# The first contraction block tile by tile, and transposes in PSUM banks of their own

## The chip, the core and the metric

The kernel runs on one core of a Trainium2 chip. The metric is the device time of one execution in microseconds; a kernel's time is the median of its runs. The core's engines run side by side, each with its own queue in program order, and meet at semaphores: TensorE (matmuls and transposes, writing to PSUM), VectorE, ScalarE, GpSimd, and SyncE (SP), which here issues all DMA transfers.

## What is computed

Inputs: x of 2048 rows by 512, and weights, all bf16. Cut to what matters, the reference is:

```python
xn = layernorm(x)
q, k, v = split(xn @ wqkv)                     # 32 heads of 16
# each row attends to 8 rows of its past, 2 apart (0, 2, ... 14 back)
logits = einsum("bhsd,bhswd->bhsw", q, kg) * 16 ** -0.5
s = einsum("bhsw,bhswd->bhsd", softmax(logits), vg) @ wo
h = gelu(xn @ w_gate) * (xn @ w_up)            # 1792 wide
out = x + s * silu(h @ w_down)
```

## The kernel before

The 2048 rows are 16 tiles of 128 rows, and 4 chunks of 4 tiles (`TQ` = 512 columns once transposed). A matmul contracts over 128 partitions, so the 512 features are 4 blocks (`NC` = 4, index `c` or `dk`), and xn is needed transposed: `xnT[j]` holds chunk j as features by rows, 4 blocks by 512 columns.

The order of the work is written out by hand. The program issues each engine's instructions in the order of the Python text, and nothing reorders them; a table of side jobs (`at`, `run`) places work of one stage between the steps of another. For each chunk j the order on TensorE is: 14 pairs of gate and up projections (`glu`), the q, k, v projections of the next chunk (`qkv`), the down projection (`down`), with the attention's sums after its first tile (`sums`: denominators, `av_sums`, then `logits` of the next chunk), and the output projection (`finish`). VectorE multiplies q by k shifted (`qk_products`, tile `pk`), E by v (`av_product`, tile `pv`) and gate by up (`h`, L452). For `av_product` of chunk 0 the v values take a way through DRAM: copied to `vst`, stored to `vT` (L295), and read back as `v_arr` by four transfers (`load_v`, L311), each for 32 of the 128 partitions.

Chunk 0 has a front of its own, which the change touches (L540 to L598):

- Transfers are issued by SP in the order x tiles 0 and 1, three of the four row blocks of wqkv (`load_wqkv`), x tiles 2 and 3, the fourth block, then more of x, and the gate and up weights.
- `first_stats`, `first_moments`, `first_rstd`, `normalize` make xn of a tile on VectorE, with the square root on ScalarE (L191).
- `to_psum` transposes xn's blocks on TensorE (L224) into one PSUM bank (tile `tr`, pool `mm` of four banks), and `from_psum` copies the bank to `xnT`, by ScalarE (L236) for tile 0 and by VectorE for tile 1, in both cases block 0 first and then the other three.
- q, k and v of chunk 0 are made in two halves of 256 columns (`HQ`). The first half (tiles 0 and 1) accumulates in six PSUM banks at once, `pairs`: two banks `v_ps`, and four of the tile `qk_ps`; each bank holds two groups of 128 outputs. These banks are zeroed by matmuls with a zero operand (L545), so that all later products only add. The loop over `dk` (L575 to L584) runs outside: 12 matmuls of 256 columns for each block, with tile 2's transposes behind block 2 and tile 3's within block 3.
- The second half (tiles 2 and 3) follows, one pair of output groups at a time (L594 to L598): `project` runs the four blocks for each of the two groups, and `copy_out` moves the bank to q, k or v.
- `warm_up` issues matmuls whose results are not used.

Of the kernel before, what the change touches and what calls it, by code (L numbers as in the profile page):

```python
# [10 lines left out]
BF16 = mybir.dt.bfloat16  # L11
F32 = mybir.dt.float32

P = 128
# [14 lines left out]
def kernel(  # L29
# [13 lines left out]
    nc = tc.nc  # L43
    B, S, D = A_x.shape
    DF = B_w_gate.shape[1]
    NT, NC, NF, NJ = S // P, D // P, DF // P, S // TQ
# [6 lines left out]
    def pool(name, bufs, **kw):  # L53
        return ctx.enter_context(tc.tile_pool(name=name, bufs=bufs, **kw))
# [19 lines left out]
    mm = pool("mm", 4, space=bass.MemoryType.PSUM)  # L74
# [4 lines left out]
    wqkv_sb = wts.tile([P, NC, 3 * D], BF16, name="wqkv_sb")  # L79
# [7 lines left out]
    def load_x(t, n=1):  # L87
        nc.sync.dma_start(
            out=x_sb[:, t : t + n, :],
            in_=x2d[t * P : (t + n) * P, :].rearrange("(t p) d -> p t d", p=P),  # L90
        )
# [7 lines left out]
    def load_wqkv(k):  # L99
        nc.sync.dma_start(out=wqkv_sb[:, k, :], in_=A_wqkv[k * P : (k + 1) * P, :])  # L100

    for t in (0, 1):
        load_x(t)
    for k in range(NC - 1):
        load_wqkv(k)
    for t in (2, 3):
        load_x(t)
    load_wqkv(NC - 1)
    load_x(TPQ, TPQ)
    for i, (lo, hi) in enumerate(((0, DF // 2), (DF // 2, DF))):  # L110
        load_w(wg_sb, B_w_gate, lo, hi)
# [19 lines left out]
    ident = const.tile([P, P], BF16, name="ident")  # L131
# [38 lines left out]
    xnT = {}  # L170
# [15 lines left out]
    def first_stats(t):  # L186
        nc.vector.bn_stats(out=stats[:, t, :], in_=x_sb[:, t, :])  # L187

    def first_moments(t):
        nc.vector.bn_aggr(out=mv[:, t, :], in_=stats[:, t, :])  # L190
        nc.scalar.activation(  # L191
            out=std[:, t, :], in_=mv[:, t, 1:2], func=AF.Sqrt, bias=epsc[:], scale=1.0
        )

    def first_rstd(t):
        nc.vector.reciprocal(out=rstd[:, t, :], in_=std[:, t, :])
# [9 lines left out]
    xns = {}  # L206

    def normalize(t, cs=range(NC)):
        if 0 in cs:
            xns[t] = xnp.tile([P, D], BF16, name="xn")  # L210
        cols = slice(cs[0] * P, (cs[-1] + 1) * P)
        nc.vector.tensor_scalar(
            out=xns[t][:, cols], in0=x_sb[:, t, cols],
            scalar1=mv[:, t, 0:1], scalar2=rstd[:, t, :],
            op0=ALU.subtract, op1=ALU.mult,
        )

    trs = {}

    def to_psum(t, cs=range(NC)):  # L220
        if 0 in cs:
            trs[t] = mm.tile([P, NC * P], BF16, name="tr", tag="mm")
        for c in cs:
            nc.tensor.transpose(  # L224
                trs[t][:, c * P : (c + 1) * P], xns[t][:, c * P : (c + 1) * P], ident[:]
            )

    def from_psum(t, cs=range(NC), copy=None):
        j, i = divmod(t, TPQ)
        if j not in xnT:  # L230
            xnT[j] = xtp.tile([P, NC, TQ], BF16, name="xnT")
        c = slice(cs[0], cs[-1] + 1)
        dst = xnT[j][:, c, i * P : (i + 1) * P]
        src = trs[t][:].rearrange("p (c n) -> p c n", c=NC)[:, c]
        if copy is None:
            nc.scalar.activation(out=dst, in_=src, func=AF.Copy)  # L236
        else:
            copy(out=dst, in_=src)

    def transpose(t, copy=None):  # L240
        to_psum(t)
        from_psum(t, copy=copy)

    def warm_up(n, cols):

        ps = mm.tile([P, TQ], F32, name="warm_ps", tag="mm")
        for _ in range(n):
            nc.tensor.matmul(
                ps[:, 0:cols], lhsT=nc.const_aps.tensor(1.0, [P, P], BF16),
                rhs=nc.const_aps.tensor(1.0, [P, cols], BF16), start=True, stop=True,  # L250
            )
# [12 lines left out]
    def project(ps, w, lo, j, i0=0, n=TQ):  # L264
        for dk in range(NC):
            nc.tensor.matmul(  # L266
                ps,
                lhsT=w[:, dk, lo : lo + P],
                rhs=xnT[j][:, dk, i0 : i0 + n],
                start=(dk == 0),  # L270
                stop=(dk == NC - 1),
            )
# [3 lines left out]
    def copy_out(j, fo, ps, i0=0, n=TQ, m=1, copy=None):  # L276

        which, c = divmod(fo, NC)
        if which == 0:
            if "q" not in st[j]:  # L280
                st[j]["q"] = qp.tile([P, NC, TQ], BF16, name="q_sb")
            dst = st[j]["q"][:, c : c + m, i0 : i0 + n]
        elif which == 1:
            dst = k_sb[j][:, c : c + m, PAD + i0 : PAD + i0 + n]
        else:
            if c // 2 not in st[j]["vst"]:
                st[j]["vst"][c // 2] = vsp.tile([P, 2, TQ], BF16, name="vst")
            dst = st[j]["vst"][c // 2][:, c % 2 : c % 2 + m, i0 : i0 + n]
        if copy is None:
            nc.scalar.activation(out=dst, in_=ps, func=AF.Copy)  # L290
        else:
            copy(out=dst, in_=ps)
        if which == 2 and (c + m) % 2 == 0 and i0 + n == TQ:
            r, lo = slice((c // 2) * 2 * P, (c // 2 + 1) * 2 * P), PAD + j * TQ
            nc.sync.dma_start(  # L295
                out=vT[r, lo : lo + TQ].rearrange("(c p) n -> p c n", p=P),
                in_=st[j]["vst"][c // 2][:],
            )
# [200 lines left out]
    for i in range(TPQ):  # L499
        at(("down", 0, 1), moments, 2 * TPQ + i)  # L500
        if i < 2:
            at(("glu", 0, i), transpose, TPQ + i)
        at(("down", 0, 2), normalize, 2 * TPQ + i)
        at(("glu", 1, 0) if i else ("down", 0, 3), transpose_by_dma, 2 * TPQ + i)
        at(("glu", 1, 10 + i), moments, 3 * TPQ + i)
        at(("qkv", 2, i), normalize, 3 * TPQ + i)
        at(("glu", 2, 0) if i else ("down", 1, 3), transpose_by_dma, 3 * TPQ + i)
# [31 lines left out]
    HQ = TPQ // 2 * P  # L539
    warm_up(6, TQ // 2)  # L540
    quad = att.tile([P, NC, 2, HQ], F32, name="qk_ps", tag="quad")
    pairs = [(8 + 2 * i, mm.tile([P, 2, HQ], F32, name="v_ps", tag="mm")[:]) for i in range(2)]
    pairs += [(2 * i, quad[:, i]) for i in range(4)]
    for _, ps in pairs:
        nc.tensor.matmul(  # L545
            ps, lhsT=zero[:], rhs=nc.const_aps.tensor(1.0, [P, 2, HQ], BF16),
            start=True, stop=False,
        )
    warm_up(4, P)
    rest = range(1, NC)  # L550
    first_stats(0)
    first_moments(0)
    first_stats(1)
    first_rstd(0)
    first_moments(1)
    normalize(0)
    to_psum(0)
    from_psum(0, [0])
    from_psum(0, rest)
    warm_up(2, P)  # L560
    first_rstd(1)
    normalize(1, [0])
    normalize(1, rest)
    to_psum(1, [0])
    from_psum(1, [0], nc.vector.tensor_copy)
    to_psum(1, rest)
    from_psum(1, rest, nc.vector.tensor_copy)
    for t in (2, 3):
        first_stats(t)
        first_moments(t)  # L570
# [1 line left out]
    for t in (2, 3):  # L572
        first_rstd(t)
        normalize(t)
    for dk in range(NC):  # L575
        for n, (fo, ps) in enumerate(pairs):
            for i in range(2):
                nc.tensor.matmul(  # L578
                    ps[:, i, :],
                    lhsT=wqkv_sb[:, dk, (fo + i) * P : (fo + i + 1) * P],  # L580
                    rhs=xnT[0][:, dk, 0:HQ],
                    start=False,
                    stop=(dk == NC - 1 and i == 1),
                )  # L584
            if (dk, n) in ((2, 5), (3, 2)):
                transpose(dk, copy=nc.vector.tensor_copy)
    for fo, ps in pairs:
        copy_out(0, fo, ps, 0, HQ, 2, nc.vector.tensor_copy if fo >= 8 else None)
    for t in range(TPQ, 2 * TPQ, 2):
# [3 lines left out]
    sum_constants()  # L593
    for n, fo in enumerate((0, 2, 4, 6, 8, 10)):  # L594
        ps = mm.tile([P, 2, HQ], F32, name="qkv_ps", tag="mm")
        for i in range(2):
            project(ps[:, i, :], wqkv_sb, (fo + i) * P, 0, HQ, HQ)
        copy_out(0, fo, ps[:], HQ, HQ, 2)  # L598
    at(("glu", 0, 0), transpose_by_dma, TPQ + 2, (0, 1))
    at(("glu", 0, 0), load_v, 0)  # L600
# [61 lines left out]
```

The softmax here doesn't subtract the row's maximum and nothing guards it: scores larger than these inputs give would overflow.

## Time and profile before

| | us |
|---|---|
| median of 6 runs | 228.74 (228.43 to 228.87) |
| the profiled execution's own time | 228.47 |
| its span, first to last instruction | 226.7 |
| TensorE matmul busy | 221.5 (98%) |
| TensorE weight loads busy | 107.0 (47%) |
| VectorE busy | 152.3 (67%) |
| ScalarE busy | 132.2 (58%) |
| GpSimd busy | 20.1 (9%) |

The profile page cuts the span into 40 slices of 5.67 us; each digit is the busy share of a slice in tenths, for PEclk the granted TensorE clock in tenths of full speed:

```profile
PE   7999999999999999999999999999999999999993
DVE  4689971999995489969812759924934448971434
PEclk9999999999999999999999999999999999999998
DMA  6999399942049911000229931100208940001002
```

In the page PE is TensorE, PEld its weight loads, DVE VectorE, ACT ScalarE, POOL GpSimd, SP the queue that issues transfers. "L224" is line 224 of the kernel before. Matmuls overlap in the pipeline, so one matmul's duration (272 ns at 256 columns) is longer than the spacing from one to the next (109 ns). The DMA row gives the mean busy share of the core's 16 transfer engines: they are saturated for most of the first 23 us, in which the weights and x arrive.

### The profile page before, as it was taken

The page shows a single profiled execution, that of the slowest core. Times are in us where ns is not written, and L with a number is a line of the kernel's source. Part 1 is how long each engine was busy: PE and PEld are TensorE (multiplying, and loading weights), DVE is VectorE, ACT ScalarE, POOL GpSimd, SP SyncE. Part 2 cuts the span into 40 slices and gives each one's busy share as a digit, 9 for nine tenths or more (in the row PEclk, how much of TensorE's full clock was granted, in tenths as well). Part 3 has the DMA queues.
Part 4 walks back from the last instruction along what each step waited for, and adds up shares of the span by engine and source line. Part 5 has one row for each costly group of instructions (what it writes and reads, how often), then busy time and mean ns, then how long its engine had stood idle before and what let it go on. Part 6 is the DMA issues. An engine that isn't in the chain of part 4 may idle for free.

```text
span 226.7 us, 3599 instructions
## 1 busy us (share of the span) xinstructions
PE 221.5 (98%) x1324; PEld 107.0 (47%) x1324; DVE 152.3 (67%) x280; ACT 132.2 (58%) x209; POOL 20.1 (9%) x67
## 2 busy tenths in 40 slices
PE   7999999999999999999999999999999999999993
PEld 3885444444444444444444444444444444444453
DVE  4689971999995489969812759924934448971434
ACT  4478679767631767676751466766763356756210
POOL 1026941000040000320000000000000000000000
PEclk9999999999999999999999999999999999999998
DMA  6999399942049911000229931100208940001002
GB/s 194 386 398 379 71 214 167 320 110 93 7 98 199 194 52 29 19 4 0 93 54 212 180 102 23 26 0 0 91 23 167 200 115 0 0 0 33 0 25 69
DMA packets 30130, 24.64 MB, mean 109 GB/s; under 512 B 10784, under 2 KB 29600, under 8 KB 30112
## 3 DMA queue, kind: packets, MB, share of 16 engines
q1 hardware_dynamic: 30112, 24.41, 44.8%
q8 instruction: 10, 0.16, 0.3%
q14 instruction: 8, 0.07, 0.1%
HBM read 18.74 MB, written 4.34 MB: 102 GB/s over the span
## 4 chain that ended last, share of the span: by engine, by line
PE 96%; DVE 1%; DMA 1%; issue 0%; ACT 0%; DVEq 0%
PE y_ps L460 21%; PE g_ps L266 21%; PE u_ps L266 21%; PE qkv_ps L266 16%; PE s_ps L476 6%; PE L_ps L355 3%; PE o_ps L423 3%; PE qk_ps L578 2%; DMA x_sb<-in_A_x_dram 1%; PE v_ps L578 1%; PE tr L224 1%; DVE stats L187 1%; PE den_ps L375 0%; DVE m L484 0%; DVE mv L190 0%
## 5 line engine op out<-in xcount | busy, mean ns | idle before, releaser
L266 PE MATMUL g_ps<-xnT,wg_sb 128*128 128x512 bf16 x224 | 57.5, 379 | 0.0
L266 PE MATMUL u_ps<-xnT,wu_sb 128*128 128x512 bf16 x224 | 57.5, 379 | 0.0
L460 PE MATMUL y_ps<-wd_sb,h 128*128 128x512 bf16 (+1 forms) x238 | 49.9, 367 | 0.0
L450 ACT ACTIVATE u<-u_ps 128x512 bf16<-128x512 f32 x56 | 33.5, 598 | 16.9 <-PE u_ps L266 16.9
L452 DVE TENSOR_TENSOR h<-ge,u 128x512 bf16<-128x512 bf16 x56 | 23.8, 425 | 29.0 <-ACT u L450 27.3
L448 ACT ACTIVATE ge<-g_ps 128x512 bf16<-128x512 f32 x56 | 33.5, 598 | 16.4 <-PE g_ps L266 16.3
L337 DVE TENSOR_TENSOR pk<-q_sb,k_sb 128x1024 bf16<-128x1024 bf16 (+1 forms) x56 | 38.9, 759 | 4.6 <-ACT k_sb L290 4.6
L409 DVE TENSOR_TENSOR pv<-E,v_arr 128x1024 bf16<-128x1024 bf16 (+1 forms) x48 | 39.7, 862 | 0.0
L266 PE MATMUL qkv_ps<-xnT,wqkv_sb 128*128 128x512 bf16 (+1 forms) x192 | 37.0, 352 | 0.0
L460 PEld LDWEIGHTS <-h 128*128 128x128 bf16 x238 | 23.0, 98 | 25.9 <-issue 1.3
L266 PEld LDWEIGHTS <-wu_sb 128*128 128x128 bf16 x224 | 21.9, 98 | 26.4
L266 PEld LDWEIGHTS <-wg_sb 128*128 128x128 bf16 x224 | 21.7, 98 | 26.3 <-issue 0.8
L468 ACT ACTIVATE sl<-y_ps 128x512 bf16<-128x512 f32 (+1 forms) x17 | 9.7, 572 | 32.6 <-PE y_ps L460 32.6
L266 PEld LDWEIGHTS <-wqkv_sb 128*128 128x128 bf16 x192 | 18.8, 98 | 17.6
L484 DVE TENSOR_TENSOR m<-s_ps,sl 128x512 bf16<-128x512 f32 (+1 forms) x17 | 11.1, 655 | 19.0 <-PE s_ps L476 19.0
L435 DVE TENSOR_TENSOR oT<-o_ps,rb 128x1024 bf16<-128x1024 f32 x8 | 9.4, 1219 | 11.8 <-DMA rb<-rs_d 6.3
L476 PE MATMUL s_ps<-wo_sb,oT 128*128 128x512 bf16 (+1 forms) x68 | 14.8, 366 | 0.0
L204 POOL TENSOR_TENSOR rstd<-rstd,mhalf 128x1 f32<-128x1 f32 x12 | 8.1, 671 | 71.2 <-DVE rstd L201 71.2
L290 ACT ACTIVATE vst<-qkv_ps 128x512 bf16<-128x512 f32 x14 | 8.4, 597 | 3.7 <-PE qkv_ps L266 3.7
L290 ACT ACTIVATE k_sb<-qkv_ps 128x512 bf16<-128x512 f32 x14 | 8.4, 601 | 3.2 <-PE qkv_ps L266 3.2
L290 ACT ACTIVATE q_sb<-qkv_ps 128x512 bf16<-128x512 f32 x14 | 8.3, 603 | 3.0 <-PE qkv_ps L266 3.0
L476 PEld LDWEIGHTS <-oT 128*128 128x128 bf16 x68 | 6.6, 98 | 7.2
(58 smaller groups left out, 126.4 us busy)
## 6 DMA issues: line engine op xcount, KB each, us to landing
v_arr<-vT SPq DMA_DIRECT2D x16, 520.0 KB, 8.6
vT<-vst SPq DMA_DIRECT2D x8, 256.0 KB, 2.5
out_dram<-o_t SPq DMA_DIRECT2D x15, 128.0 KB, 2.5
wg_sb<-in_B_w_gate_dram SPq DMA_DIRECT2D x2, 896.0 KB, 9.9
wu_sb<-in_B_w_up_dram SPq DMA_DIRECT2D x2, 896.0 KB, 10.8
wd_sb<-in_B_w_down_dram SPq DMA_DIRECT2D x1, 1792.0 KB, 10.7
wqkv_sb<-in_A_wqkv_dram SPq DMA_DIRECT2D x4, 384.0 KB, 4.7
x_sb<-in_A_x_dram SPq DMA_DIRECT2D x3, 512.0 KB, 9.8
```

The costliest lines, as they stand in the source:

```text
L266: nc.tensor.matmul(ps, lhsT=w[:, dk, lo : lo + P], rhs=xnT[j][:, dk, i0 : i0 + n], start=(dk == 0), stop=(dk == NC - 1),)
L290: nc.scalar.activation(out=dst, in_=ps, func=AF.Copy)
L337: nc.vector.tensor_tensor(out=st[j]["pk"][w][:, c0 : c0 + n, :], in0=st[j]["q"][:, c0 : c0 + n, :], in1=k_sb[j][:, c0 : c0 + n, off : off ...
L409: nc.vector.tensor_tensor(out=pv[:, d : d + n, :], in0=st[j]["E"][:, wh, :].unsqueeze(1).to_broadcast([P, n, TQ]), in1=st[j]["va"][:, 4 * ...
L435: nc.vector.tensor_tensor(out=oT[:, g : g + 2, :], in0=st[j]["o"][:, g : g + 2, :], in1=st[j]["rb"][:].unsqueeze(1).to_broadcast([P, 2, TQ ...
L448: nc.scalar.activation(out=ge[:], in_=g_ps[:], func=AF.Gelu_apprx_tanh)
L450: nc.scalar.activation(out=u[:], in_=u_ps[:], func=AF.Copy)
L452: nc.vector.tensor_tensor(out=h[:], in0=ge[:], in1=u[:], op=ALU.mult)
L460: nc.tensor.matmul(y[:], lhsT=st[j][fc][:, tt * P : (tt + 1) * P], rhs=wd_sb[:, fc, cols], start=(fc == 0), stop=(fc == NF - 1),)
L468: nc.scalar.activation(out=sl[:], in_=y[:], func=AF.Silu)
L476: nc.tensor.matmul(s[:], lhsT=st[j]["oT"][:, g, tt * P : (tt + 1) * P], rhs=wo_sb[:, g, cols], start=(g == 0), stop=(g == NC - 1),)
L484: nc.vector.tensor_tensor(out=m[:], in0=s[:], in1=sl[:], op=ALU.mult)
```

## The change

The products of block 0 are made for tile 0 alone and then for tile 1 alone, 128 columns each, in place of 256 columns at once. They are put between the transposes of tile 1. To that end tile 0's normalization is split like tile 1's was, and block 0's transposes of both tiles go into one PSUM bank (`tra`), those of the other three blocks into another (`trb`). Two unused matmuls go. The transposes of tiles 2 and 3 move to later places in block 3. The first pair of output groups of the second half is made tile by tile too. The load loop is written out with the same transfers in the same order.

```diff
-    for t in (0, 1):
-        load_x(t)
-    for k in range(NC - 1):
-        load_wqkv(k)
-    for t in (2, 3):
-        load_x(t)
-    load_wqkv(NC - 1)
+    load_x(0)
+    load_x(1)
+    load_wqkv(0)
+    load_wqkv(1)
+    load_wqkv(2)
+    load_x(2)
+    load_x(3)
+    load_wqkv(3)
...
-    def to_psum(t, cs=range(NC)):
-        if 0 in cs:
-            trs[t] = mm.tile([P, NC * P], BF16, name="tr", tag="mm")
-        for c in cs:
+    def to_psum(t, cs, tr):
+        for n, c in enumerate(cs):
             nc.tensor.transpose(
-                trs[t][:, c * P : (c + 1) * P], xns[t][:, c * P : (c + 1) * P], ident[:]
+                tr[:, n * P : (n + 1) * P], xns[t][:, c * P : (c + 1) * P], ident[:]
             )
...
+    def block(dk, ns, i0=0, n=HQ):
+        for b in ns:
+            fo, ps = pairs[b]
+            for i in range(2):
+                nc.tensor.matmul(
+                    ps[:, i, i0 : i0 + n],
+                    lhsT=wqkv_sb[:, dk, (fo + i) * P : (fo + i + 1) * P],
+                    rhs=xnT[0][:, dk, i0 : i0 + n],
+                    start=False,
+                    stop=(dk == NC - 1 and i == 1),
+                )
+
+    one, rest = [0], range(1, NC)
+    tra = mm.tile([P, 2, P], BF16, name="tra", tag="mm")
+    trb = mm.tile([P, 2, (NC - 1) * P], BF16, name="trb", tag="mm")
     first_stats(0)
     first_moments(0)
     first_stats(1)
     first_rstd(0)
     first_moments(1)
-    normalize(0)
-    to_psum(0)
-    from_psum(0, [0])
-    from_psum(0, rest)
-    warm_up(2, P)
+    normalize(0, one)
+    to_psum(0, one, tra[:, 0])
+    from_psum(0, one, tra[:, 0])
+    normalize(0, rest)
+    to_psum(0, rest, trb[:, 0])
+    from_psum(0, rest, trb[:, 0])
     first_rstd(1)
-    normalize(1, [0])
+    normalize(1, one)
     normalize(1, rest)
-    to_psum(1, [0])
-    from_psum(1, [0], nc.vector.tensor_copy)
-    to_psum(1, rest)
-    from_psum(1, rest, nc.vector.tensor_copy)
+    block(0, range(2), 0, P)
+    to_psum(1, one, tra[:, 1])
+    from_psum(1, one, tra[:, 1], nc.vector.tensor_copy)
+    block(0, range(2, 6), 0, P)
+    to_psum(1, rest, trb[:, 1])
+    from_psum(1, rest, trb[:, 1], nc.vector.tensor_copy)
+    block(0, range(6), P, P)
...
-    for dk in range(NC):
-        for n, (fo, ps) in enumerate(pairs):
-            for i in range(2):
-                nc.tensor.matmul(
-                    ps[:, i, :],
-                    lhsT=wqkv_sb[:, dk, (fo + i) * P : (fo + i + 1) * P],
-                    rhs=xnT[0][:, dk, 0:HQ],
-                    start=False,
-                    stop=(dk == NC - 1 and i == 1),
-                )
-            if (dk, n) in ((2, 5), (3, 2)):
-                transpose(dk, copy=nc.vector.tensor_copy)
+    block(1, range(6))
+    block(2, range(6))
+    block(3, range(3))
+    transpose(2, nc.vector.tensor_copy)
+    block(3, range(3, 5))
+    transpose(3, nc.vector.tensor_copy)
+    block(3, range(5, 6))
...
     for n, fo in enumerate((0, 2, 4, 6, 8, 10)):
         ps = mm.tile([P, 2, HQ], F32, name="qkv_ps", tag="mm")
-        for i in range(2):
-            project(ps[:, i, :], wqkv_sb, (fo + i) * P, 0, HQ, HQ)
+
+        w = HQ if n else P
+        for i0 in range(0, HQ, w):
+            for i in range(2):
+                project(ps[:, i, i0 : i0 + w], wqkv_sb, (fo + i) * P, 0, HQ + i0, w)
         copy_out(0, fo, ps[:], HQ, HQ, 2)
```

## The prediction

> **What bounds the kernel.** I read the chain of waits first, by line and in order of time, then the timeline of the first 13 us for each engine, then TensorE's later waits. TensorE carries the end:
>
> ```profile
> PE 96%; DVE 1%; DMA 1%; issue 0%; ACT 0%; DVEq 0%
> ```
>
> It can therefore be shortened only before TensorE's stream starts, or where the stream pauses. The chain in order of time shows the start of the stream (start us, us, what):
>
> ```profile
> 5.25 0.33 DVE xn L212
> 5.57 0.04 issue
> 5.62 0.24 PE tr L224
> 5.86 0.02 issue
> 5.89 0.24 DVE xnT L238
> 6.12 0.04 issue
> 6.17 0.33 PE tr L224 x3
> ...
> 59.34 1.77 PE L_ps L355 x32
> ...
> 113.24 1.73 PE L_ps L355 x32
> ```
>
> Up to 6.17 TensorE serves as one link in tile 1's chain: normalize, transpose, copy, transpose. The first product starts at 6.33 in the timeline, behind all transposes of tiles 0 and 1. From there every step of the chain is TensorE's. So the change is worth what its stream of first products gains on the present one, less what a later stage takes back. For the latter, note that the logits of chunk 1 (L_ps at 59.34) take 1.77 us and those of chunk 2, the same 32 instructions, 1.73.
>
> **The front, step by step.** Durations are those of the early timeline and of the groups by shape.
>
> Tile 0. Its normalization starts at 4.60 as now. In place of one 128x512 operation (382 ns) comes a 128x128 one, then 128x384. Tile 1 has both shapes: 314 and 374 ns, the second starting 0.23 after the first. The first ends at 4.92. TensorE starts 0.05 after its data (4.98 to 5.04 now) and a transpose takes 0.23: 4.97 to 5.20. Now ScalarE's copy waits for all four:
>
> ```profile
> 5.04 0.40 PE L224 MATMUL tr<-ident,xn 128*128 128x128 bf16 x4 [0.53 <-DVE xn L212]
> ...
> 5.48 0.66 ACT L236 ACTIVATE xnT<-tr 128x128 bf16<-128x128 bf16 x2 [0.46 <-PE tr L224]
> ```
>
> (start us, us, engine, line, operation, out<-in, shape, count, idle time before; 5.04 + 0.40 = 5.44, copy at 5.48.) With block 0 in its own bank it waits for one: 5.24, 278 ns, 5.52. The first product follows at **5.57**, for 6.33 now. Its weights landed at 1.71 + 3.3 = 5.0.
>
> From there TensorE runs 4 products, 1 transpose, 8 products, 3 transposes, 12 products before block 1: 28 instructions of 128 columns. Their spacing is the price that decides. In the fence above four transposes, each with a weight load of its own, take 0.40 with a single one at 0.23: (0.40 - 0.23)/3 = 0.056. So 28 x 0.0555 = 1.55, and block 1 starts at 7.13. Now it starts at 7.64 (6.33 + 12 x 0.109). **Gain 0.51.**
>
> Waits inside, each against its slot: rstd of tile 1 is pushed by the extra VectorE operation from 5.05 to about 5.13, so xn block 0 of tile 1 ends at 5.64 and the rest at 5.93. TensorE comes to that transpose at 5.80 (cover 0.1; without it 0.08 is lost). Its copy ends at 6.29, wanted at 6.46. ScalarE's second copy ends at about 6.11, wanted at 6.30 by tile 1's other transposes. Their copy ends at 6.63 + 0.04 + 0.36 = 7.03, wanted at 7.13: the tightest, 0.05 after the signal. Weights of blocks 1, 2, 3 land at 6.6, 7.6, 9.2, wanted at 7.13, 8.44, 9.74. The stall at 6.17, 0.32 behind VectorE's copy of the shared bank, and the wait for four transposes both go; what is late next is TensorE itself. The two removed warm-ups (0.11) lie in an idle stretch, and the pause before the transposes shrinks. The load loop written out issues the same eight transfers.
>
> Tiles 2 and 3. Their normalization ends at 10.15 and 10.67 as now (the x tiles land at 7.9 and 8.3). TensorE gets to tile 2 at 7.13 + 30 x 0.109 = 10.39 and to tile 3 at 10.39 + 0.22 + 0.44 = 11.05, so the later places cover the earlier stream. Then 2 products end at 11.49. The first group pair starts with tile 2, whose copy ends at 10.82 + 0.42 = 11.24. Tile 3's copy ends at 11.47 + 0.42 = 11.89, its part starts at 11.94. As one 256-column pair it would wait until 11.94 to start at all, 0.45 lost; that is what the split is worth. It has 16 instructions of 128 columns for 8 of 256: 0.89 for 0.87. The next pair starts at 12.40 where now it is 12.91: **0.51 stays**. ScalarE's copies shift along. VectorE's next stretch moves only 0.09, as its casts follow tile 3's copy, but at 25.5 it waits for ScalarE's u (0.23 idle), and the last pk before the first L_ps ends at 32.27 with TensorE there at 33.36: covered.
>
> **Where part of it stops.** The transfers do not move. The last quarter of v_arr is issued at 28.09 and:
>
> ```profile
> DMA to landing us min/median/max: 12.0/12.0/12.0
> ```
>
> It lands at 40.1, and the first pv starts at 40.27:
>
> ```profile
> 39.93 0.43 DVE L452 TENSOR_TENSOR h<-ge,u 128x512 bf16<-128x512 bf16 x1 [0.55 <-ACT u L450]
> 40.27 1.22 DVE L409 TENSOR_TENSOR pv<-E,v_arr 128x2048 bf16<-128x2048 bf16 x1
> 41.41 0.42 DVE L452 TENSOR_TENSOR h<-ge,u 128x512 bf16<-128x512 bf16 x1
> 41.74 1.22 DVE L409 TENSOR_TENSOR pv<-E,v_arr 128x2048 bf16<-128x2048 bf16 x1
> 43.01 0.43 DVE L452 TENSOR_TENSOR h<-ge,u 128x512 bf16<-128x512 bf16 x1
> 43.35 1.22 DVE L409 TENSOR_TENSOR pv<-E,v_arr 128x2048 bf16<-128x2048 bf16 x1
> 44.73 0.43 DVE L452 TENSOR_TENSOR h<-ge,u 128x512 bf16<-128x512 bf16 x1 [0.17 <-ACT u L450]
> 45.08 5.76 DVE L409 TENSOR_TENSOR pv<-E,v_arr 128x2048 bf16<-128x2048 bf16 x5
> 50.75 9.71 DVE L337 TENSOR_TENSOR pk<-q_sb,k_sb 128x1024 bf16<-128x1024 bf16 x16
> ```
>
> With h half a us earlier, pv still has to wait for 40.1. From 40.27 VectorE can go at its own pace: pv to h 1.14, h to pv 0.33. That gives h at 41.41, 42.88, 44.35 and the run of five pv at 44.69 for 45.08. The pk behind it have no gap, so the last ends at 60.07 for 60.46 (50.75 + 9.71): **0.39 earlier, no more**. The 28th of the 32 L_ps instructions needs it, and TensorE waits there by 0.04 already (1.77 against 1.73). So TensorE cannot leave that stage more than 0.39 earlier, and everything behind follows it. The transfer's own range: the two vT rows that v_arr waits for are issued at 17.2 and 18.1, would be issued 0.5 earlier, and take 7.1 and 7.9 us to land, where chunk 1's take 2.8 and 4.0. They queue behind the input loads; if so, nothing moves. At the other end they move by the full 0.5, for which speaks that the transfers' share between 23 and 26 us is only 0.26. I take 0, as the queueing is the larger part. SP gets no other order.
>
> **Rule against row.** The Trainium skill, "TensorE: Matmul & The Clock Gate", section on the back-to-back issue gap, says that in streams of weight load and matmul pairs 128 columns cost about 81 ns each, not 56. The change makes 12 pairs of 256 columns into 24 of 128 and 8 into 16, so it adds the overhead of 20 instructions and must not pay more than half a 256-column slot each. By the row the 40 short ones cost 40 x 0.0555 = 2.22, by the rule 3.24. The rule takes the 0.51 away and adds another 0.5. The row has loads at the same spacing through six instructions (transposes and warm-ups, 5.05 to 5.33), so a load hides behind a 128-column matmul. I take the row. The load's own 98 ns is the far end.
>
> **Sum.** Profiled execution: 228.47, span 226.7 (1.77 around it). Span 226.31, time 228.08. Against the median, 228.74 - 0.39 = **228.35**.
>
> **Rivals.**
> - *All comes through*: v_arr lands earlier with its vT rows, or in most executions. Then 0.51 + the 0.04 of the present wait: 228.20. For it: half-idle transfers before 26. Against: the saturated queue up to 23.
> - *Little comes through*: v_arr lands 0.3 to 0.4 later than in this one profile. Then pv binds before and after alike: 228.6 to 228.74. For it: the six runs spread 0.44. Against: nothing in the change adds transfers. The same time results if the products start late because a copy is waited for as a whole (first product at 6.16, block 1 at 7.7).
> - *Slower*: short pairs bound by weight loads. At 81 ns 40 x 0.0255 = +1.02, less 0.51, less the 0.04 wait that then vanishes: 229.2. At 98 ns +1.70: 229.9. It decides from 0.0555 + 0.55/40 = 69 ns per pair. Against it stands the row above; for it that no run of more than six such loads is in the trace.
>
> **Chances.** A difference of 0.2% is 0.46 us, about what can be told from no change. Main case 0.42 (0.25 to 0.5 gained, 228.25 to 228.5; about a third of it beyond 0.46), all comes through 0.32, little 0.11, slower 0.15. Faster 0.15 + 0.29 = 0.44, same 0.42, slower 0.14. Range 228.0 to 229.0: it takes in the first three and leaves out most of the slower one.
>
> **What would show it.** First v_ps product near 5.57 and block 1 near 7.13; 128-column products spaced 55 to 57 ns; the second pair of the second half near 12.40; pv not before 40.2 with idle VectorE ahead of it; L_ps of chunk 1 at 1.85 to 1.9 us. Wrong if the short products are spaced over 69 ns, if v_arr moves with TensorE, or if a wait appears between 7 and 12 us.

## The result and the profile after

| kernel | runs | median us | lowest to highest | ratio to the kernel before, 95% interval |
|---|---|---|---|---|
| before | 40 | 228.76 | 228.35 to 229.39 | 1 |
| after | 20 | 228.13 | 227.79 to 228.61 | 0.9976 [0.9970, 0.9982] |

By the ratio, the changed kernel is 0.55 us faster (0.41 to 0.69); the medians lie 0.63 apart. The forecast was 228.35, a gain of 0.39. This lies just below the interval; the rival "all comes through" (0.51 to 0.55) lies in it.

The profiled execution of the changed kernel took 228.35 with a span of 226.6, only 0.12 less than the profiled execution of before (228.47, 226.7). So this pair of profiles shows a fifth of what the medians show, and the first question was where the rest is. The chain of waits, by engine:

```profile
PE 98%; DVE 0%; issue 0%; DVEq 0%
```

It was 96% with 1% each for VectorE and DMA: nearly the whole chain is TensorE's own work. In order of time (start us, us, what), read from the profiled execution of after:

```profile
4.84 0.43 PE warm_ps L245 x4
5.26 0.11 PE tra L221
5.37 0.43 PE trb L221 x3
5.80 0.32 PE v_ps L551 x4
6.12 0.06 PE tra L221
6.17 0.45 PE qk_ps L551 x8
6.62 0.17 PE trb L221 x3
...
10.52 0.22 PE qk_ps L551 x2
10.74 0.02 issue
10.76 0.40 PE tr L221 x4
...
59.21 1.77 PE L_ps L352 x32
```

Three readings. First, normalization and copies no longer appear between the first transposes and the products: the stall ahead of tile 1's transposes is gone. Second, the four warm-ups take 0.43 and the three transposes behind them 0.43, where three later ones take 0.17. TensorE ran at half its rate until shortly before the first product. The two timelines show it too, first before, then after (start us, us, engine, line, operation, out<-in, shapes, count):

```profile
2.92 1.36 PE L545 MATMUL qk_ps<-const-bfloat16-1.0,zero 128*128 128x512 bf16 x4
4.12 0.40 PE L248 MATMUL warm_ps<-const-bfloat16-1.0 128*128 128x128 bf16 x4
```

```profile
2.92 1.91 PE L542 MATMUL qk_ps<-const-bfloat16-1.0,zero 128*128 128x512 bf16 x4
4.63 0.63 PE L245 MATMUL warm_ps<-const-bfloat16-1.0 128*128 128x128 bf16 x4
```

The same four zeroing matmuls, which the change leaves alone, take 1.36 in one execution and 1.91 in the other, so the difference is one between executions. Third, tile 2's transposes start at 10.76, 0.18 after TensorE is free (an "issue" of 0.02 stands in the chain; the timeline shows the gap): tile 2 of x landed at 8.48 in this execution and at 7.92 in the one of before. Both chances fell on the changed kernel. A second profiled execution of each kernel, the two on one chip, makes another pair (the clock's rise is read from the trace's record of the granted clock):

| times in us | before | before, second | after | after, second |
|---|---|---|---|---|
| TensorE's clock rises to full | 3.6 | 5.2 | 5.7 | 4.2 |
| x tile 2 landed | 7.92 | 8.27 | 8.48 | 8.35 |
| first product | 6.33 | 6.37 | 5.74 | 5.54 |
| block 1 starts | 7.64 | 7.68 | 7.31 | 7.12 |
| second pair of second half starts | 12.91 | 13.21 | 12.78 | 12.64 |
| v_arr landed | 40.13 | 40.26 | 39.19 | 39.89 |
| first pv starts | 40.27 | 40.57 | 40.14 | 40.02 |
| L_ps of chunk 1 starts | 59.34 | 59.64 | 59.21 | 59.07 |
| span | 226.74 | 227.06 | 226.62 | 226.49 |

Read down the second and fourth columns: 0.57 is gained by the second pair, 0.57 is still there at L_ps, and 0.57 in the span. In the first and third columns it is 0.13, 0.13 and 0.12. Nothing that is gained or lost in the front is given back later, in either pair. Neither pair is quite even: in the second one chance favours the changed kernel, as the clock rises earlier in it and tile 2's transposes wait for their rows for 0.15, for 0.25 in before.

TensorE's timeline of the second execution of after, for the steps that were predicted:

```profile
5.54 0.40 PE L551 MATMUL v_ps<-xnT,wqkv_sb 128*128 128x128 bf16 x4
...
7.12 0.60 PE L551 MATMUL v_ps<-xnT,wqkv_sb 128*128 128x256 bf16 x4
...
10.63 0.40 PE L221 MATMUL tr<-ident,xn 128*128 128x128 bf16 x4
...
11.30 0.39 PE L221 MATMUL tr<-ident,xn 128*128 128x128 bf16 x4
...
11.74 1.50 PE L263 MATMUL qkv_ps<-xnT,wqkv_sb 128*128 128x128 bf16 x20
```

From the first product to block 1 it is 1.58 for 28 instructions of 128 columns: 56 ns each. In the first pair of the second half, 16 short instructions from 11.74 to 12.64 give 56 again.

And VectorE's timeline of the same execution, where the prediction saw the gain capped:

```profile
39.66 0.43 DVE L449 TENSOR_TENSOR h<-ge,u 128x512 bf16<-128x512 bf16 x1 [0.56 <-ACT u L447]
40.02 1.23 DVE L406 TENSOR_TENSOR pv<-E,v_arr 128x2048 bf16<-128x2048 bf16 x1
...
44.47 0.42 DVE L449 TENSOR_TENSOR h<-ge,u 128x512 bf16<-128x512 bf16 x1 [0.17 <-ACT u L447]
44.81 5.76 DVE L406 TENSOR_TENSOR pv<-E,v_arr 128x2048 bf16<-128x2048 bf16 x5
```

The first pv starts 0.36 after h starts. In before it is 0.34, so a wait for v_arr can be 0.02 at most. The brackets name ScalarE's u as what VectorE waited for, still as in before. The cap did not bind.

### The profile page after: what moved, and what is told of

Same layout as the page of the kernel before. It is cut to its first block, busy times and chain, and to the rows that moved or that the text cites. A ratio compares the mean times of both kernels' runs of the same rounds, so it can differ in the third digit from the quotient of the medians.

```text
span 226.6 us, 3637 instructions
## 1 busy us (share of the span) xinstructions
PE 222.3 (98%) x1342; PEld 107.6 (47%) x1342; DVE 152.3 (67%) x281; ACT 132.3 (58%) x209; POOL 21.4 (9%) x67
## 4 chain that ended last, share of the span: by engine, by line
PE 98%; DVE 0%; issue 0%; DVEq 0%
PE y_ps L457 21%; PE g_ps L263 21%; PE u_ps L263 21%; PE qkv_ps L263 16%; PE s_ps L473 6%; PE L_ps L352 3%; PE o_ps L420 3%; PE qk_ps L551 2%; PE warm_ps L245 1%; PE v_ps L551 1%; PE qk_ps L542 1%; PE tr L221 0%; PE den_ps L372 0%; PE v_ps L542 0%; PE trb L221 0%; DVE m L481 0%
## 5 line engine op out<-in xcount | busy, mean ns | idle before, releaser
L263 PE MATMUL qkv_ps<-xnT,wqkv_sb 128*128 128x512 bf16 (+2 forms) x200 | 37.0, 345 | 0.0
```

The costliest lines, as they stand in the source:

```text
L263: nc.tensor.matmul(ps, lhsT=w[:, dk, lo : lo + P], rhs=xnT[j][:, dk, i0 : i0 + n], start=(dk == 0), stop=(dk == NC - 1),)
```

## The experiments

Two theories were held against each other. By the **stream** theory, the gain is the front's (a product stream that starts earlier and stays dense), and it reaches the end. By the **landing** theory, the landing of v_arr cuts it off near 0.39; the expectations call this the cap theory. Four kernels, u1 to u4, undo one part of the change each, the v and c kernels move the landing, and i1 tries to go further. Each ratio is to runs of before taken beside the kernel: their median was 228.73 for a0 and u1 to u3, 228.79 for u4, v1, v2 and i1, and 228.55 for c0, c1, a1 and b1. No kernel puts back the two removed matmuls by themselves.

**The changed kernel again, beside its parts (a0).** No edit.

> The changed kernel once more, as it is, for a second profile of it. Stream theory (the start of TensorE's stream sets the end and nothing later takes any back): 0.50 to 0.55 us under the kernel before. Cap theory (v_arr's landing near 40 us holds pv, and the L_ps of chunk 1 gives back what is over 0.39): 0.35 to 0.40 under it, L_ps of chunk 1 at 1.85 us or more. Clock theory (in the first profile of the changed kernel the TensorE clock rose at 5.7 us where in that of before it rose at 3.6, which is chance of the execution): with a rise before 4.5 us the first product lies near 5.57 and block 1 near 7.13; with a late rise near 5.75 and 7.3.

Measured: 228.22 (11 runs), ratio 0.9981 [0.9972, 0.9989], a gain of 0.43 (0.25 to 0.64). Its first product came at 5.73 and its second half started at 11.82, with the clock's rise at 6.1. The two measurements of the changed kernel overlap; 0.39 is in this interval and 0.51 too. The medians of one kernel alone do not tell the two theories apart.

**Block 0 whole (u1).** The banks, the split of tile 0 and the split pair stay; the products of block 0 wait for both tiles.

```diff
-    block(0, range(2), 0, P)
     to_psum(1, one, tra[:, 1])
...
-    block(0, range(2, 6), 0, P)
     to_psum(1, rest, trb[:, 1])
...
-    block(0, range(6), P, P)
+    block(0, range(6))
```

> Block 0 again in products of 256 columns behind all transposes of tile 1; banks, split normalization, later transposes and the pair by tiles stay. Stream theory: tile 1's three transposes share a bank with tile 0's and wait for ScalarE's second copy (6.11), so block 0 starts at 6.3 and block 1 at 7.6 as before: no gain, 0.5 us slower than the changed kernel, ratio to before 1.000. If instead the banks and the later transposes bring the gain by themselves, it stays 0.4 to 0.5 under the kernel before.

Measured: 228.54, ratio 0.9994 [0.9986, 1.0002], not told apart from before: 0.14 of the gain is left, 0.32 at most. TensorE's timeline:

```profile
5.59 0.22 PE L221 MATMUL tra<-ident,xn 128*128 128x128 bf16 x1
6.13 0.33 PE L221 MATMUL trb<-ident,xn 128*128 128x128 bf16 x3 [0.32 <-ACT xnT L232]
6.30 0.60 PE L551 MATMUL v_ps<-xnT,wqkv_sb 128*128 128x256 bf16 x4
...
7.61 0.60 PE L551 MATMUL v_ps<-xnT,wqkv_sb 128*128 128x256 bf16 x4
```

The first product is back at 6.30 and block 1 at 7.61, beside 6.33 and 7.64 in before. The 0.32 of idle time is there again under another name: in before VectorE's copy of tile 1's block 0 held the shared bank, here it is ScalarE's copy of tile 0's other blocks, which uses the same bank trb. In the changed kernel the products of the first tile lie in this gap. So in this profile the new banks bring the products no earlier unless the first tile's products stand between the transposes.

**Banks by tile (u4).** Everything of the change stays but the layout: one bank for each tile in place of one for block 0 and one for the rest.

```diff
-    tra = mm.tile([P, 2, P], BF16, name="tra", tag="mm")
-    trb = mm.tile([P, 2, (NC - 1) * P], BF16, name="trb", tag="mm")
+    tr0 = mm.tile([P, NC * P], BF16, name="tr0", tag="mm")
+    tr1 = mm.tile([P, NC * P], BF16, name="tr1", tag="mm")
...
-    to_psum(0, one, tra[:, 0])
+    to_psum(0, one, tr0[:, 0:P])
...
-    to_psum(0, rest, trb[:, 0])
+    to_psum(0, rest, tr0[:, P:])
```

> The transposes of each tile again in a bank of the tile's own (four blocks in one bank) in place of block 0 and the others apart; the order of all instructions stays as in the changed kernel. Stream theory: tile 0's other transposes wait for ScalarE's copy of block 0 (5.57), tile 1's others for VectorE's (6.55), so block 1 starts near 7.4 in place of 7.13: half of the gain stays, 0.25 under the kernel before. If the banks don't matter: 0.5 to 0.55 under it.

Measured over 21 runs: 228.40, ratio 0.9989 [0.9982, 0.9995], a gain of 0.25 (0.11 to 0.41): about half of the whole change. TensorE's timeline shows the place:

```profile
5.73 0.38 PE L221 MATMUL tr<-ident,xn 128*128 128x128 bf16 x3 [0.37 <-ACT xnT L232]
5.95 0.39 PE L551 MATMUL v_ps<-xnT,wqkv_sb 128*128 128x128 bf16 x4
```

The three other transposes of tile 0 wait 0.37 for ScalarE's copy of block 0 from the same bank, and the first product starts at 5.95 behind them, beside 5.54 to 5.74 in the changed kernel. The split and the banks are two halves of one thing. In every kernel here a tile of transposes fills a bank of its own, so no run tells whether it is the bank or the tile that is waited for.

**The first pair whole (u2).**

```diff
-        w = HQ if n else P
+        w = HQ
```

> The first pair of output groups of the second half again with 256 columns; all else of the change stays. Stream theory: the pair waits for tile 3's copy at 11.94 in place of 11.49; TensorE idles 0.45 us there, the kernel stays 0.05 to 0.1 under the one before. Cap theory: the loss against the changed kernel is only 0.3, as that one has 0.39 at most to lose. If tile 3's copy is not late, no loss.

Measured: 228.48, ratio 0.9996 [0.9988, 1.0004], a gain of 0.09 left, 0.27 at most. TensorE's timeline:

```profile
11.75 0.38 PE L551 MATMUL qk_ps<-xnT,wqkv_sb 128*128 128x256 bf16 x2
12.43 1.80 PE L263 MATMUL qkv_ps<-xnT,wqkv_sb 128*128 128x256 bf16 x15 [0.30 <-DVE xnT L234]
```

Two products from 11.75 at 0.109 end at 11.97, and the pair starts at 12.43, behind VectorE's copy of tile 3: 0.46 lost, where the prediction had 0.45. With a later place for the transposes and no split, most of the front's gain is lost at the seam, where the second half begins.

**Transposes at their old places (u3).** Tile 2 goes back ahead of block 3, tile 3 to behind three pairs of it.

```diff
-    block(3, range(3))
     transpose(2, nc.vector.tensor_copy)
-    block(3, range(3, 5))
+    block(3, range(3))
     transpose(3, nc.vector.tensor_copy)
-    block(3, range(5, 6))
+    block(3, range(3, 6))
```

> Tile 2's transposes again behind block 2 and tile 3's behind the third pair of block 3; all else of the change stays. Stream theory: TensorE reaches tile 2's transposes at 9.74, its normalized rows are there at 10.20 (x lands at 7.9, later in the first profile of the changed kernel, 8.5), so it idles 0.45 to 0.9 us: 0 to 0.1 under the kernel before, or above it by up to 0.3 where x lands late. If x of tile 2 is early enough in most executions, no loss.

Measured: 228.64, ratio 0.9998 [0.9989, 1.0006].

```profile
10.20 0.40 PE L221 MATMUL tr<-ident,xn 128*128 128x128 bf16 x4
...
11.96 1.28 PE L263 MATMUL qkv_ps<-xnT,wqkv_sb 128*128 128x128 bf16 x18
```

In this execution x came early enough that TensorE waited only 0.09 for tile 2, and the second half started at 11.96 with the clock's rise at 6.2, within 0.14 of the changed kernel's 11.82 at 6.1. The profile thus shows less of a loss than the runs do, by whose ratio most of the gain is lost (0.05 left, 0.25 at most). In the executions with later x, this order waits longer: before has the same places, and its second execution waited 0.25 there. That this makes up the whole difference is argued from the landings, not measured.

**The landing taken away (v1 on before, v2 on after).** Chunk 0's v is read from x, an input, in place of the stored vT, so that its transfers wait for no store. Chunk 0's attention output is then not the reference's.

```diff
-                    tensor=vT.tensor,
+                    tensor=vT.tensor if j else A_x.tensor,
...
-                    ap=[[SV * DH, H], [SV, DH], [1, VW]],
+                    ap=[[(SV if j else S - PAD) * DH, H], [SV if j else S - PAD, DH], [1, VW]],
```

> The kernel before, with chunk 0's v_arr read from the input x in place of the stored v (same rows and bytes; so chunk 0's attention output is not the reference's). It does not wait for the stored v and lands some 3 us sooner, near 37. Both theories: the kernel before waits for v_arr only in executions where it lands after 40.2; if that is rare, ratio 1.000; if it is frequent, up to 0.1 us faster.

> The changed kernel with the same: chunk 0's v_arr read from x (chunk 0's attention output is not the reference's), landing near 37. Cap theory: the cap goes, 0.1 to 0.15 us faster than the changed kernel, 0.55 and more under the kernel before. Stream theory (v_arr is in time in most executions): same as the changed kernel within 0.05.

Measured: v1 228.68, ratio 0.9996 [0.9988, 1.0004]; v2 228.06 (6 runs), ratio 0.9971 [0.9959, 0.9982]. v_arr landed at 38.05 and 37.66, some two us sooner than in before, where three were expected. In before that is worth nothing that can be measured. In the changed kernel it is worth 0.0005 of the ratio against the first measurement and 0.001 against the second (0.1 to 0.2 us), inside the intervals. So if the landing takes a part of the gain at all, it is a small one.

v2's profile is also the cleanest front of all: clock's rise at 4.3, x tile 2 at 7.96, first product 5.41, tile 2's transposes at 10.25 without a wait, second pair at 12.26, span 226.10. Against before's second pair at 12.91 that is 0.65, and the spans differ by 0.64. (0.13 of it is tile 0 of x, which landed at 2.83 and not at 2.96.)

**The landing delayed (c0 on before, c1 on after).** SP's queue is reordered so that v_arr of chunk 0 is issued behind more of the transposing transfers.

```diff
-    at(("glu", 0, 0), transpose_by_dma, TPQ + 2, (0, 1))
+    at(("glu", 0, 0), transpose_by_dma, TPQ + 2)
+    at(("glu", 0, 0), transpose_by_dma, TPQ + 3, (0, 1))
     at(("glu", 0, 0), load_v, 0)
-    at(("glu", 0, 0), transpose_by_dma, TPQ + 2, (2, 3))
-    at(("glu", 0, 0), transpose_by_dma, TPQ + 3)
+    at(("glu", 0, 0), transpose_by_dma, TPQ + 3, (2, 3))
```

> The kernel before, with four of the six DMA transposes of tiles 6 and 7 ahead of chunk 0's v_arr transfers in place of behind them, so that v_arr is issued some 2 us later. Cap theory (pv waits for v_arr, and from there VectorE's chain to the L_ps of chunk 1 holds TensorE): with the last quarter landing at A, the first pv is at A + 0.14, the run of five pv 4.4 later, and TensorE waits before or in L_ps of chunk 1 for what this exceeds 45.1; for a landing at 41.5 some 0.9 us slower than the kernel before. If TensorE does not depend on it: ratio 1.000.

> The changed kernel with the same move. Cap theory: both are bound by v_arr, whose landing does not follow TensorE, so the gain is gone: the same time as the kernel before with this move, within 0.15 us. If TensorE does not depend on v_arr's landing, or the landing follows TensorE's earlier start: 0.5 us under that one, as without the move.

Measured: c0 230.67 (6 runs, 229.73 to 231.84), ratio 1.0096 [1.0069, 1.0123]; c1 229.88 (5 runs, 229.60 to 230.13), ratio 1.0057 [1.0044, 1.0070]. VectorE's timeline of c0, then of c1:

```profile
41.95 1.23 DVE L409 TENSOR_TENSOR pv<-E,v_arr 128x2048 bf16<-128x2048 bf16 x1 [1.65 <-DMA v_arr<-vT]
...
46.37 5.75 DVE L409 TENSOR_TENSOR pv<-E,v_arr 128x2048 bf16<-128x2048 bf16 x5
```

```profile
42.08 1.22 DVE L406 TENSOR_TENSOR pv<-E,v_arr 128x2048 bf16<-128x2048 bf16 x1 [1.81 <-DMA v_arr<-vT]
...
46.50 5.76 DVE L406 TENSOR_TENSOR pv<-E,v_arr 128x2048 bf16<-128x2048 bf16 x5
```

Now the bracket ahead of pv names the transfer. In both kernels pv starts 0.12 after the landing (41.83, 41.96), the run of five pv follows 4.42 later as predicted, and TensorE waits in L_ps: from den_ps to the next y_ps it takes 5.07 and 5.24, where every other profile has 3.73. TensorE's timeline of c0 shows the waits:

```profile
59.11 1.87 PE L355 MATMUL L_ps<-pk,dsum 128*32 128x512 bf16 x26
61.20 0.38 PE L355 MATMUL L_ps<-pk,dsum 128*32 128x512 bf16 x1 [0.23 <-DVE pk L337]
61.81 0.59 PE L355 MATMUL L_ps<-pk,dsum 128*32 128x512 bf16 x5 [0.23 <-DVE pk L337]
```

The chain of c0's page:

```profile
PE 80%; DVE 10%; DMA 6%; SPq 2%; issue 1%; ACT 0%; DVEq 0%; ACTq 0%
```

VectorE and the DMA have come into it. Span minus landing is 186.2 in both, so in this pair of executions the front's gain is gone and the landing alone sets the end. So the cap is real as a mechanism. The medians do not show the two kernels equal within 0.15, as they should be under a binding landing: 0.79 lies between them, with few runs and intervals that just touch. The traced execution of c0 (229.73) is the fastest of its six, and the median is 2.1 above that of before where 0.9 was expected of a landing at 41.5. Only one execution of each has a trace, so whether the landings differ by as much in the others stays open.

**x sooner (i1).** An attempt to go further: tiles 2 and 3 of x are loaded ahead of the third block of wqkv, so that tile 2's transposes need not wait.

```diff
     load_wqkv(1)
-    load_wqkv(2)
     load_x(2)
     load_x(3)
+    load_wqkv(2)
     load_wqkv(3)
```

> The changed kernel with x tiles 2 and 3 loaded ahead of wqkv's third block. They land some 1.0 us sooner, the third block 0.7 later (7.8 to 8.3, wanted at 8.4). If TensorE waits for tile 2's rows in many executions (0.18 idle at 10.76 in the first profile of the changed kernel), 0.1 to 0.2 us faster than the changed kernel and 0.6 to 0.75 under the one before; if that was chance, the same as the changed kernel; if the third block is late, slower by up to 0.3.

Measured: 228.58 (13 runs, 228.0 to 231.65, the slowest not in the ratio), ratio 0.9996 [0.9984, 1.0007]: 0.09 of the gain is left, 0.37 at most. Tile 2's transposes did not wait (11.10, straight behind the products). But the execution profiled has the latest clock rise of all, 6.8, and the first product itself waited for its weights, as the weight loads (LDWEIGHTS) show:

```profile
5.79 0.35 PEld L551 LDWEIGHTS <-wqkv_sb 128*128 128x128 bf16 x4 [0.27 <-DMA wqkv_sb<-in_A_wqkv_dram]
```

The first block of wqkv landed at 5.75, although it is issued ahead of what was moved. The third landed at 8.74; here block 2 starts at 9.13, but in an execution like the second one of after it would be wanted near 8.4 and TensorE would wait some 0.3. Whether that is what the runs show, or the late first block is, stays open.

**Both kernels profiled again (b1, a1).** No edit; their numbers are in the table above.

> The kernel before as it is, for a second profile of it. Clock theory (the moment at which the TensorE clock rises is chance of the execution): with a rise after 5 us, its first product lies near 6.6 and its span near 227.0, where the first profile, with a rise at 3.6, has 6.33 and 226.7. If the rise is a property of the kernel, it is at 3.6 again.

> The changed kernel as it is, for a third profile. With a rise of the clock before 4.5 us: first product 5.4 to 5.6, block 1 near 7.0 to 7.1, span near 226.1. With a late one: 5.75, 7.3 to 7.5, 226.5. v_arr's last quarter: near 39.2 again if its landing follows the stores of v, 39.1 to 40.1 if it is chance.

Measured: 228.79 and 228.19, one execution each, 0.60 apart; spans 227.06 and 226.49. The fronts are 0.57 apart, and so are the ends. Single executions scatter: 11 runs of before beside these two have a median of 228.55. Two expectations missed. In b1 the clock rose at 5.2 and the first product came at 6.37, not near 6.6; its span of 227.06 comes from the wait of 0.25 for tile 2. In a1 the span is 226.49, not 226.1, in part as TensorE waited 0.07 for block 3's weights (landed at 9.76) and 0.15 for tile 2. With v_arr at 39.89 in a1, pv started 0.13 after it, where c0 and c1, which do wait, have 0.12: here the landing only just did not bind.

## Why the prediction was right, and where it was not

- **The start.** First product predicted at 5.57; 5.54 with an early clock rise, 5.73 and 5.74 with late ones. Right for executions whose clock rises early; the prediction took the clock of one execution as given.
- **The spacing.** Predicted 55 to 57 ns; 56 in 28 and in 16 instructions in a row. The row of four transposes held for long runs, and the rival "slower", which decides from 69, falls. By the rule of 81 (the Trainium skill, "TensorE: Matmul & The Clock Gate", back-to-back issue gap) block 1 would have started, as an estimate, at 5.54 + 28 x 0.081 = 7.81; it started at 7.12.
- **Tiles 2 and 3.** Transposes predicted at 10.39 and 11.05 with no wait; measured 10.63 and 11.30 in a1, with a wait of 0.07 for block 3's weights (they landed at 9.76, not at 9.2) and one of 0.15 for tile 2; the first profile has 0.18 for tile 2. "A wait between 7 and 12 us" was named as a sign against the forecast. It came, because tile 2 of x landed at 8.35 and 8.48 and not at 7.92. It takes little of the gain, as before waits too when x is late (0.25 in its second execution). In v2, where x landed at 7.96, there is no wait.
- **The seam** between the halves. The split of the first pair was put at 0.45; undoing it (u2) left 0.46 idle. Second pair predicted at 12.40; measured 12.64 and 12.78, and 12.26 in v2. Against before the difference is 0.13 and 0.57 in the two pairs. The most alike executions are v2 and the first of before: 0.65, and 0.52 without the 0.13 of tile 0's earlier landing, where 0.51 was forecast.
- **The cap: the mis-sized term.** The sum took 0.39 of the 0.51, since v_arr lands at 40.13, and "I take 0" for what its landing moves. The mechanism is right: c0 and c1 show pv tied to the landing, 4.42 to the run of five, and TensorE waiting in L_ps. The size was taken from one landing in one execution. In three executions of the changed kernel v_arr landed at 39.14 to 39.89. With the latest of these the cap lies at 0.39 + (40.13 - 39.89) = 0.63, above what the front brings. The first pv came at 40.02 to 40.14 and L_ps of chunk 1 took 1.77, where "not before 40.2" and 1.85 to 1.9 were named as signs. The traces show the way: v_arr's first transfer is issued 0.06 to 0.07 after the last vT row has landed, at 25.02 to 25.55 in the three and at 25.70 and 25.98 in before. That row is issued a little earlier in the changed kernel (17.83 to 17.97, for 18.10 and 18.40), but its time to land differs between executions of one kernel by as much (7.05 to 7.72, and 7.30 and 7.88). How much of the earlier landing is the change's and how much chance stays open.
- **A small one.** The rival "all comes through" added 0.04 for a wait that TensorE has in L_ps now. In v2 v_arr landed at 37.66 and L_ps of chunk 1 still took 1.78: that 0.04 is not a wait for v_arr.

So the direction, the spacing and the front's sum were right, and the case that came is the rival in which all comes through. It was luck that the clock and the landings of x, which the sum took from one execution, mattered little to the difference of the medians: each moves a single execution by some 0.2 to 0.3. The range of 228.0 to 229.0 takes in no change at all too, so that 228.13 lies in it says little; the traces carry the argument.

## What to carry to other kernels

Where one engine's stream sets the end, a stream that starts half a us earlier is worth half a us only if each later seam is moved with it: undoing any one of three edits lost most of the gain. Before a transfer's landing is used as a cap, look at a second execution: it moved here by more than the margin that decided. The same goes for a comparison of profiles, where one pair showed 0.12 and another 0.57 of a change that the ratio puts at 0.55.

## What the runs showed of the hardware

**TensorE's clock rises at a time of its own.** In fourteen profiles of this program and its variants the rise lay between 3.6 and 6.8 us after the start, although TensorE's work begins at 0.83 or 0.84 in all of them and is the same in its first 12 matmuls, the last of which starts at 3.9 to 4.2. Until it, 128-column matmuls are 107 ns apart, and 56 after it. The record of the clock starts at the rise, so the clock row of the page shows a 9 from its first slice on, and the slow start is seen only in the early timeline. In the kernel before, a rise at 5.7 (v1) goes with a first product at 6.62 and a span of 227.04, one at 3.6 with 6.33 and 226.74: some 0.3 us, as large as half of the change. The runs without a trace support it in part. Full speed lasted 221.87 us in thirteen of the profiles and 225.28 in the other, 3.41 more, and half speed follows; so in before only an early rise brings the mean granted clock of a run below 1.000. Of 94 runs of before, 29 have that. They are 0.2 us faster in two of the three sets of runs (83 runs) and no faster in the third (11). The Trainium skill ("TensorE: Matmul & The Clock Gate", Part 1) describes a clock that starts at half and is released by a window of activity of about 3.4 us that runs freely, so that its phase is one of chance. The half rate, the chance and the step of 3.41 us agree with these traces; the spread of 3.2 us is within one such window, but wider than the half us either way that it gives.

**Landings differ between executions by as much as the change is worth.** The same transfer in the same place of its queue landed at 7.7 to 8.5 (tile 2 of x, in the executions of the table and those of a0, v1 and v2), 4.7 to 5.75 (first block of wqkv) and 39.1 to 40.3 (v_arr of before and after).
